# Turning the last three pairs' inputs by DMA, whole-run loads for a range test, and a new instruction order

## The chip, the core and the metric

The kernel runs on one core of one Trainium2 chip. A core has engines with a queue each, which run side by side and wait for one another through semaphores: TensorE (PE: matrix products, with its weight loads shown as PEld), VectorE (DVE), ScalarE (ACT) and GpSimd (POOL); SyncE (SP) issues DMAs here. Each queue is worked off in order: an instruction that waits holds up all that stand behind it on its engine. The metric is the device time of the program in microseconds (us), as the median of the runs.

## The reference

Two blocks follow one another. The first is a gated linear attention with complex gates, for 4 batches, 8 heads, 768 tokens and head width 48:

```python
mag = np.sqrt(a_re * a_re + a_im * a_im)
scale = np.minimum(mag, 0.999) / (mag + 1e-06)
a_re_n, a_im_n = (a_re * scale, a_im * scale)
for t in range(S):
    new_re = ar * S_re - ai * S_im
    new_im = ar * S_im + ai * S_re
    S_re, S_im = (new_re + kv, new_im)        # kv = outer product of k[t] and v[t]
    y[:, :, t] = np.einsum('bhd,bhde->bhe', q[:, :, t], S_re)
```

Its output, with the heads side by side (384 columns), is x of a mixer: `h = x^T U V` mixes along the tokens through rank 32, `u = x + h^T`, and the result is `u + relu(u w1) w2` with 1536 hidden columns. The weights come in as float64, the rest as float32.

## The kernel before

**Work and stages.** The recurrence is done in 24 chunks of 128 tokens, 6 for each batch, and two neighbouring chunks are a group (12 groups). For a group, `gates` (L690) computes from a_re and a_im the logarithms of the magnitudes and the angles, sums them along the tokens with TensorE (`within`, L777; `angles`, L842), and makes scale factors (es) and cosines and sines (cs). The phase at the end of a chunk is carried into the next one of its batch: in batch 0 by TensorE, later (from chunk 7 on) by a small adding DMA on POOL's queue (L828, "gate<-F" in the profile), behind which VectorE's cast of L836 waits. `prep` (L880) multiplies q and k by these. From chunk 6 on (`ACROSS`) `cross` (L919) turns the products by DMA: ScalarE splits each 32-bit word into two 16-bit planes (L932), SP writes them to DRAM (L933), and a transposing DMA reads them back (L934). `chain` (L938) does the chunk's attention: inner products (L956), key-value states (L976), outputs (L1005, L1013), into the tile xo of the chunk.

When the six chunks of a batch are through, `mixer` (L1029) runs for its three pairs of chunks (12 pairs in all, m = 0 to 11). The rank products (L1048) of the batch are kept by ScalarE as r (L1054). For a pair, `spread` (L1063) multiplies r by V into two banks of PSUM (L1071, one TensorE operation for both chunks), `mixed` (L1076) adds them to xo on VectorE, and `turned` (L1080) turns xo for the up-projection: three transposes on TensorE for each chunk (L1087), and one copy out of PSUM into the tile uT (L1091). uT has two buffers. Pair 0 is turned and up-projected ahead of its batch's end, and a correction by the rank (`ranked`, L1116 and L1124, with ScalarE's copy at L1128, and `corrected`, L1142) brings in the mixing later. Its weights and those of the other pairs come in as 64-bit words, which ScalarE and VectorE make into 32-bit ones in passes (`single`, L589) in the first 110 us or so. From pair 2 on the up-projection is `up_fewer` (L1163): sums of blocks of uT on VectorE (L1186), then 15 groups of 8 TensorE instructions ("few" and "bank", L1214), with copies and additions of the parts on ScalarE and VectorE. `down_two` (L1311) does the down-projection in 14 halves of 6 instructions (L1346), adds to xo (L472) and sends the result out (L1290).

**The range test.** The fast path holds for a range of the gates alone. `again` (L665) reads a_re and a_im a second time for every group, into the places that the gates have left: four loads by SP (two arrays, two chunks, 128 tokens x 8 heads x 48 values in runs of 192 bytes; L671), a square on ScalarE (L674), and two VectorE operations (`ranged`, L658: L660 and L661) that leave a count in `bad`; `low` is a place to write for the second. `judge` (L1480) looks at the counts at the end. The test needs every value once, in any arrangement.

**What sets the order.** The program is planned before it is emitted. Each call of `PE`, `ACT`, `DVE`, `POOL` or `SP` enters an operation with what it reads and writes; the buffers are taken and given back by the plan (`takes`, rings). The tuple `ORDER` then lists all 2276 operations by their number in the order in which they are emitted, and so fixes the order in each engine's queue. `SPARE` and `WARM` add matmuls without a use ahead of the operations they name (L1506, L1513). The costs, `late`, `way` and `steps` in these calls are notes for whoever makes ORDER; they do not reach the program.

Of the kernel before, what the change touches and what calls it, by code (L numbers as in the profile page):

```python
# [10 lines left out]
FP = mybir.dt.float32  # L11
# [8 lines left out]
CH = 128  # L20
# [98 lines left out]
)  # L119

SPARE = {
    410: 3, 447: 1,
}

WARM = {
# [201 lines left out]
def kernel(  # L327
# [125 lines left out]
    def SP(cost, *a, **kw):  # L453
        plan.add("SP", 0.63, *a, late=cost, **kw)
# [1128 lines left out]
```

## Time and profile before

| | |
|---|---|
| median of 3 runs | 530.15 us (529.94 to 530.81) |
| the profiled execution | 529.77 us |
| its span, first to last instruction | 528.0 us |
| mean granted TensorE clock | 0.997 |
| busy: PE, DVE, ACT, POOL | 509.3, 414.5, 346.0, 31.6 us |
| HBM read and written | 43.03 and 23.63 MB |

The page of the profile gives busy times, groups of instructions by line with their mean duration in ns, the idle time ahead of them and what ended it, and the chain of waits: from the last instruction back, at each step to what released it. Matmuls are pipelined: the mean duration of one is longer than the time by which it moves the chain on, so for TensorE the pieces of the chain (start, length, what) are read, not the means. Times in rows are us from the start of the span unless ns stands beside them. A busy TensorE need not be at its peak.

### The profile page before, as it was taken

The numbers are of one execution on the slowest core, as the hardware profiler recorded it, in microseconds if no ns is written. First come the engines' busy times: TensorE is split into PE (matmuls) and PEld (weight loads), VectorE is DVE, ScalarE is ACT, GpSimd is POOL, SyncE is SP. The second block draws the span as 40 slices with busy tenths as digits, with TensorE's granted clock in tenths as the row PEclk, the third lists the DMA queues.
The fourth block names the chain that finished last, engine by engine and source line by source line (L and its number), as shares of the span: only waits on it lengthen the run. The fifth ranks groups of instructions, "written<-read, shape, count | busy, mean of one in ns | idle before, by whom it ended". The sixth has DMA issues, their size and how long they took to land.

```text
span 528.0 us, 15692 instructions
## 1 busy us (share of the span) xinstructions
PE 509.3 (96%) x6670; PEld 460.3 (87%) x6670; DVE 414.5 (79%) x787; ACT 346.0 (66%) x555; POOL 31.6 (6%) x61
## 2 busy tenths in 40 slices
PE   4999999899999999999999999999999999999996
PEld 2777887666998997999999989999999989999996
DVE  4779897799989987898798797878796575958452
ACT  8899998998869978978896768843543313131100
POOL 1000000001010000101011000110000000000110
PEclk9999999999999999999999999999999999999998
DMA  9959958479999998999899958999897543333101
GB/s 226 173 115 270 209 115 191 140 138 217 197 215 244 216 215 145 204 217 202 205 198 227 210 144 175 170 242 229 192 217 178 108 90 61 76 60 61 39 32 35
DMA packets 280670, 87.06 MB, mean 165 GB/s; under 512 B 271288, under 2 KB 272784, under 8 KB 280592
## 3 DMA queue, kind: packets, MB, share of 16 engines
q1 hardware_dynamic: 278384, 81.63, 76.0%
q0 software_dynamic: 2208, 4.35, 2.4%
q8 instruction: 54, 0.88, 0.7%
q14 instruction: 24, 0.20, 0.1%
HBM read 43.03 MB, written 23.63 MB: 126 GB/s over the span
## 4 chain that ended last, share of the span: by engine, by line
PE 88%; ACT 5%; DMA 3%; DVE 2%; issue 1%; SPq 0%; ACTq 0%
PE down L1346 25%; PE few L1214 14%; PE bank L1214 11%; PE up L1102 6%; PE inner L956 4%; PE bank L1013 4%; PE bank L976 4%; PE down L1303 3%; PE bank L1005 2%; DMA gate<-F 2%; PE bank L1071 2%; PE bank L1087 2%; ACT gate L466 1%; PE bank L777 1%; PE bank L782 1%; PE bank L842 1%
## 5 line engine op out<-in xcount | busy, mean ns | idle before, releaser
L466 ACT ACTIVATE gate<-gate 128x768 f32<-128x768 f32 (+2 forms) x85 | 86.1, 1018 | 25.8 <-DMA gate<-in_a_im_dram 14.7
L1346 PE MATMUL down<-w,h 128*128 128x192 f32 x396 | 70.4, 328 | 0.0
L466 ACT ACTIVATE QK<-QKC 128x768 uint16<-128x768 uint16 (+1 forms) x72 | 58.5, 848 | 13.1 <-DVE QKC L469 7.9
L1346 PEld LDWEIGHTS down<-w,h 128*128 128x128 f32 x396 | 64.6, 190 | 1.2 <-issue 0.8
L469 DVE TENSOR_TENSOR QKC<-qk,cs 128x768 f32<-128x768 f32 x48 | 44.9, 952 | 1.0 <-ACT cs L466 0.6
L472 DVE TENSOR_TENSOR xo<-down,xo 128x192 f32<-128x192 f32 (+1 forms) x79 | 29.9, 385 | 14.3 <-PE down L1346 14.1
L1222 ACT COPY h<-few 128x512 f32<-128x512 f32 x35 | 20.2, 583 | 27.8 <-PE few L1214 27.6
L1222 ACT COPY h<-bank 128x512 f32<-128x512 f32 x25 | 14.3, 588 | 36.0 <-PE bank L1214 31.0
L1346 PE MATMUL down<-stage 128*128 128x192 f32 x198 | 37.2, 328 | 0.0
L1102 PE MATMUL up<-uT,w 128*128 128x256 f32 x144 | 33.8, 383 | 0.0
L1346 PEld LDWEIGHTS down<-stage 128*128 128x128 f32 x198 | 32.5, 190 | 0.3 <-issue 0.2
L1102 PEld LDWEIGHTS up<-uT,w 128*128 128x128 f32 x144 | 26.7, 190 | 4.9 <-issue 0.6
L1290 POOL DMA_DIRECT2D out_dram<-xo x32 | 18.5, 590 | 202.9 <-DVE xo L472 164.5
L463 ACT ACT_TABLE_LOAD x22 | 28.2, 1283 | 1.1 <-PEq L1567 0.7
L828 POOL DMA_DIRECT2D gate<-F x15 | 12.0, 797 | 274.7 <-DVE stage L616 86.3
L1226 DVE CUSTOM_DVE_ANT_1 h<-few,h 128x512 f32<-128x512 f32 x31 | 21.0, 686 | 8.8 <-PE few L1214 8.1
L1214 PE MATMUL few<-extra,w 128*128 128x128 f32 x216 | 27.8, 275 | 0.0
L956 PE MATMUL inner<-QK 112*64 112x64 f32 x768 | 27.5, 224 | 0.2 <-DVE AT L959 0.2
L466 ACT ACTIVATE cs<-F 128x384 f32<-128x384 f32 x48 | 24.4, 518 | 3.9 <-DVE F L851 3.7
L956 PEld LDWEIGHTS inner<-QK 112*64 112x64 f32 x768 | 24.5, 138 | 2.4 <-issue 0.8
L1214 PEld LDWEIGHTS few<-extra,w 128*128 128x128 f32 x216 | 26.3, 192 | 0.1
L466 ACT ACTIVATE es<-bank 128x384 f32<-128x384 f32 x44 | 18.4, 502 | 9.2 <-PE bank L777 8.2
(185 smaller groups left out, 1166.8 us busy)
## 6 DMA issues: line engine op xcount, KB each, us to landing
xd<-QK SPq DMA_DIRECT2D x36, 512.0 KB
gate<-in_a_re_dram SPq DMA_DIRECT2D x48, 192.0 KB
gate<-in_a_im_dram SPq DMA_DIRECT2D x48, 192.0 KB
stage<-in_moe_w_ch_dram SPq DMA_DIRECT2D x12, 768.0 KB
qk<-in_q_dram SPq DMA_DIRECT2D x24, 192.0 KB
qk<-in_k_dram SPq DMA_DIRECT2D x24, 192.0 KB
VP<-in_v_dram SPq DMA_DIRECT2D x24, 192.0 KB
out_dram<-xo POOLq DMA_DIRECT2D x12, 192.0 KB, 4.2
```

Source lines behind the costliest of these rows:

```text
L463: ACT(1.37, rank, lambda: nc.scalar.preload_act_table_set(name), writes=[TABLE])
L466: return nc.scalar.activation(out=o, in_=i, func=f, **kw)
L469: nc.vector.tensor_tensor(out=o, in0=a, in1=b, op=OP.mult)
L472: nc.vector.tensor_tensor(out=o, in0=a, in1=b, op=OP.add)
L956: nc.tensor.matmul(out=get(*ps0)[r:r + HC, h], lhsT=k_of(h, r, HC), rhs=q_of(h, r, HC), start=True, stop=True, tile_position=(0, r))
L976: nc.tensor.matmul(out=get(*dk[r])[x:x + D, h], lhsT=get(*ks)[at, h, x // DP, 0:D], rhs=get(*VPi)[at, h], start=True, stop=True, tile_posi ...
L1013: nc.tensor.matmul(out=get(*y[u])[side(r, u), p], lhsT=q_of(h, r * HC, HC), rhs=get(*(mid_G if r else ("G", i - 1)))[:, h], start=False, s ...
L1102: nc.tensor.matmul(out=get(*ps)[:, e], lhsT=w1[:, f, (ff + e) * 128:(ff + e + 1) * 128], rhs=get(*uT)[:, f], start=(f == 0), stop=(f == KD ...
L1214: nc.tensor.matmul(out=get(*ps)[:, q], lhsT=w()[:, q * 128:(q + 1) * 128], rhs=v[0](), start=(n == 0 and q == 0), stop=True, skip_group_ch ...
L1222: ACT(c_act(n3 * CH) - 0.045, RU, lambda i=i, k=k: nc.scalar.copy(out=at(i, k), in_=get(*ps)), [ps], [o])
L1226: DVE(c_dve(n3 * CH), RU, lambda i=i, k=k: nc.vector._custom_dve(dve_ops.TENSOR_ADD_SAT, out=at(i, k), in0=get(*ps), in1=at(i, k), s0=math ...
L1346: nc.tensor.matmul(out=get(*to)[:, part], lhsT=x(j), rhs=y[:, j], start=(first and j == 0), stop=(j == KH - 1), skip_group_check=not first)
```

## The change

Four things change. For the pairs m = 9, 10 and 11 (chunks 18 to 23) `turned` calls the new `across`: two ScalarE operations split xo into 16-bit planes in XU (one tile, a ring of one buffer), SP writes the planes to DRAM (six places) and issues a transposing DMA that writes the chunk's part of uT. Their three transposes and the copy go. `again` loads a group's a_re and a_im with one DMA each, in runs of 3072 bytes, and `low` holds 16-bit numbers. The operation of `spread` no longer takes a buffer of uT; the turn does. ORDER is a new list of 2264 operations, with other SPARE and WARM.

```diff
 ORDER = (
...
 SPARE = {
-    410: 3, 447: 1,
+    403: 1, 410: 1, 416: 1, 422: 1, 447: 1,
 }
 WARM = {
-    112: (2, 1), 126: (1,), 136: (2, 2, 2, 2, 2, 2, 1), 141: (2,), 162: (2, 2, 2), 235: (2, 2, 2, 2, 1), 242: (2,), 245: (2,), 259: (2, 2, 1), 266: (1, 1, 1, 1, 1, 1, 1, 1, 1),
+    125: (2, 2, 1), 126: (1,), 136: (2, 2, 2, 2, 2, 2, 1), 140: (2, 2), 163: (2, 1), 187: (2,), 201: (1,), 235: (2, 2, 1), 239: (2,), 242: (2,), 245: (2, 1), 259: (2, 2, 2, 1, 1, 1, 1, 1), 263: (1,),
 }
...
-    low = singles.tile([128, GC * DM], FP, name="low")
+    low = singles.tile([128, GC * DM], U16, name="low")
+    XU = singles.tile([128, 2, DM], U16, name="XU")
...
+    TURNED = (9, 10, 11)
...
-        for (nm, src), i in ((a, i) for a in ((ar, a_re), (ai, a_im)) for i in range(lo, hi)):
-            SP(c_dma(DM), ("load", 30 + n), lambda nm=nm, src=src, i=i: nc.sync.dma_start(out=get(*nm)[:, i - lo], in_=rows(src, i)),
-               writes=[nm + (i,)])
         flat4 = lambda a: get(*a).rearrange("p c h d -> p (c h d)")
+        b, c = where(lo)
+        for nm, src in ((ar, a_re), (ai, a_im)):
+            SP(c_dma(W), ("load", 30 + n), lambda nm=nm, src=src: nc.sync.dma_start(
+                out=flat4(nm), in_=src[b, :, c * CH:(c + hi - lo) * CH].rearrange("h t d -> h (t d)").rearrange("h (p m) -> h p m", m=W)), writes=[nm])
...
-            PE(0.76, R0, products, [r, ("V", 0)] + [uT + ("kept",)] * (m >= AHEAD), ps, way=5, steps=8)
+            PE(0.76, R0, products, [r, ("V", 0)], ps, way=5, steps=8)
...
+            if m in TURNED:
+                across(cc, i, u)
+                return
...
-            PE(0.33, R0, turn, [u], [tr], steps=KD)
+            PE(0.33, R0, turn, [u], [tr], takes=[uT], steps=KD)
...
+        def across(cc, i, u):
+            xu, xv = ("xu", i), ("xv", i)
+            ring(xu, "xu", [XU])
+            buffer(xv, "XV", 6, [CH, DM], bass.MemoryType.DRAM)
+            for n in range(2):
+                ACT(c_act(DM), R0, lambda n=n: act(get(*xu)[:, n], get(*u).bitcast(U16).rearrange("p (m n) -> p m n", n=2)[:, :, n], AF.Copy),
+                    [u], [xu + (n,)])
+            SP(0.6, R0, lambda: nc.sync.dma_start(out=get(*xv).bitcast(U16), in_=get(*xu).rearrange("p n m -> p (n m)")), [xu], [xv])
+            SP(0.8, R0, lambda: nc.sync.dma_start_transpose(
+                out=get(*uT).rearrange("p f (c t) -> p f c t", c=MC)[:, :, cc].bitcast(U16),
+                in_=get(*xv).bitcast(U16).rearrange("t (n m) -> (t n) m", n=2)), [xv], [uT + (cc,)])
```

Where the new order puts things that matter here: behind the rank products of batch 3 come one group of pair 8's up-projection, pair 9's mixing products, three more such groups, the mixing products of pairs 10 and 11, and twelve halves of pair 8's down products, and then pair 9's first up-projection group. Pair 9's transposing DMAs, the write of chunk 20 and the transposing DMA of chunk 20 stand on SP in that order with two range loads among them. Behind the rank products of batch 1 come two state products (L976) ahead of the mixing products. In batch 0 an up product (L1102) that stood between the rank products and L1116 is now earlier.

174 rows, old and new, of the table ORDER are left out of this document.

## The prediction

> **What bounds the kernel now.** I read the page first, then the waits of TensorE, then the stages, then the chain of waits.
>
> ```profile
> PE 509.3 (96%) x6670; PEld 460.3 (87%) x6670; DVE 414.5 (79%) x787; ACT 346.0 (66%) x555; POOL 31.6 (6%) x61
> ```
>
> TensorE (PE) is busy for 96% of the 528.0 us. A busy PE can still stand and wait behind a pipelined matmul, so the waits come next (total, times, longest, in us).
>
> ```profile
> PE bank L782 <- DVE GL L742: 7.7, 1, 7.7
> PE up L1142 <- ACT more L1128: 2.1, 1, 2.1
> PE down L1346 <- DVE xo L472: 1.1, 1, 1.1
> PE down L1346 <- DVE stage L1338: 0.7, 1, 0.7
> PE bank L1071 <- ACT r L1054: 0.6, 1, 0.6
> ```
>
> The 7.7 us are the start, before there is anything to multiply. After that four waits are worth naming, 4.5 us in all. That is all that a better order can win back from idle PE; more has to come from less PE work.
>
> ```profile
> 0.00:40.00 40.00, 31.14 (x287) 22.33 (x288) 26.28 (x51) 35.02 (x57) 1.94 (x14) 1.00 0.87 172
> 40.00:80.00 40.00, 39.96 (x815) 32.19 (x813) 35.70 (x56) 38.73 (x71) 0.00 (x0) 1.00 0.85 200
> ...
> 440.00:480.00 40.00, 40.00 (x319) 39.55 (x318) 27.50 (x61) 9.57 (x17) 0.54 (x1) 1.00 0.42 77
> ```
>
> The columns are the stage and its length, then PE, PEld, DVE, ACT and POOL busy, the granted clock (1.00: nothing more to be had there), the DMA share, GB/s. There are three regimes: up to 40 us ScalarE (35.02 of 40) sets the pace; from 40 us PE does, with ScalarE almost as full (38.73); late, PE alone is full, and ScalarE (9.57) and the DMA engines (0.42) have room.
>
> The chain of waits agrees: from 284 us to the last down products it is PE, piece upon piece; the rows of (1) are some of them (start, us, what). A PE instruction removed late shortens the span by its own length, as long as nothing new makes PE wait.
>
> **The change part by part.** (1) **Six turns leave PE.** Chunks 18 to 23 lose their three transposes each. These are the six in the chain, between pieces of other work that I need below:
>
> ```profile
> 431.79 0.33 PE bank L1087 x3
> 432.12 0.98 PE down L1346 x6
> 433.10 0.33 PE bank L1087 x3
> ...
> 445.43 0.33 PE bank L1087 x3
> 445.76 0.89 PE few L1214 x8
> ...
> 453.07 0.85 PE bank L1071 x8
> 453.92 0.48 PE bank L1087 x3
> ...
> 465.94 0.66 PE bank L1087 x6
> ```
>
> 0.33 + 0.33 + 0.33 + 0.48 + 0.66 = 2.13 us, all on the chain: **-2.1 us**. [...]
>
> What comes instead: two ScalarE splits for each chunk, and two DMAs on SP's queue. The nearest rows are a ScalarE pass over 384 columns, the mixing addition, the stores of tokens (96 and 192 KB; one chunk's write to DRAM is 192 KB too), and the transposing DMAs that the kernel has already (8 blocks each, the new ones have 3):
>
> ```profile
> L466 ACT ACTIVATE cs<-F 128x384 f32<-128x384 f32 x48 | 24.4, 518 | 3.9 <-DVE F L851 3.7
> ```
> ```profile
> L472 DVE TENSOR_TENSOR xo<-bank,xo 128x384 f32<-128x384 f32 x24 | 12.8, 551 | 4.0 <-issue 2.3 <-PE bank L1071 1.7
> ```
> ```profile
> L1290 POOL DMA_DIRECT2D out_dram<-xo x32: 539/539/859, 127.7 to 509.7; - x32
> ...
> DMA to landing us min/median/max: 1.9/3.5/6.1
> ```
> ```profile
> L934 SPq DMA_TRANSPOSE QK<-xd x36: 1732/2794/4559, 119.3 to 407.5; - x36
> ```
>
> ScalarE gains 12 x 0.52 us and loses six copies of about 0.48: +3.4 us, in a stage where it has 30 of 40 us free: nothing. The latency matters. XU is one buffer, so the second chunk's splits wait until the first chunk's write has landed. For pair 9, from the end of its mixing products: addition 0.55, splits 1.04, write 3.5, splits 1.04, write 3.5, transposing DMA about 1.0 (3/8 of 2.79) to issue and 3.5 to land, two small additions at most 0.6: 14.7 us. The transposing DMA's landing does not show in the trace; I give it the stores' median, and bound it by 1.9 and 6.1. The cover is counted in the new order: between these products and pair 9's first up-projection PE has three "few" groups (0.89), two more mixing products (0.85) and twelve halves of pair 8's down products (0.98): 2.7 + 1.7 + 11.8 = 16.2 us. So it is hidden with 1.5 us to spare; each us beyond that is a us of PE. Queued behind on SP are range loads, which nobody on the path waits for; behind the blocked splits on ScalarE stand range squares, and pair 9's own copies. Pairs 10 and 11 have over 25 us of PE between their mixing and their first use. Their transposes stand behind range loads on SP, which wait for the test before (DVE), but 15 us or more of PE lies there too. Cost: 0, from both sides -0 and +7 (all three landings at 6.1 give 22.5).
>
> (2) **Range tests.** 48 loads become 24 of the same bytes in long runs.
>
> ```profile
> L671 SPq DMA_DIRECT2D gate<-in_a_re_dram x24: 367/582/1881, 319.6 to 477.7; - x24
> ```
>
> The first is issued at 319.6 us, where PE has no wait left, so the saved DMA time is worth 0; it only keeps SP freer for (1). The test's output in 16 bits changes a DVE instruction off the path: 0, bounds 0.
>
> (3) **The mixing products no longer take the uT buffer.** They may run earlier, and do: pairs 10 and 11 are mixed right after pair 9. It adds no work; two PSUM banks are held longer, at a time when the chains of the last pairs use others. 0.
>
> (4) **The new order.** Two waits above come from one mechanism:
>
> ```profile
> 151.00 6.34 DMA gate<-F
> ...
> 157.37 0.37 DVE GS L836
> ```
> ```profile
> 275.81 6.09 DMA gate<-F
> ```
> ```profile
> DMA to landing us min/median/max: 1.9/3.9/6.3
> ```
>
> The phase carried from chunk to chunk is added by a DMA (L828; last fence: its landings). VectorE stands at the cast behind it, and what PE needs is queued there. In the old order PE has only 2.9 us of its own work between chunk 10's phase and chunk 11's cast, 2.8 before chunk 17's. The new order puts 4.9 and 7.3 us there. But chunks 7, 19 and 21 come down to 3.7 to 3.9, less than the landing's median of 3.9 alone. Of 1.1 + 0.7 = 1.8 us I count **-1.2**; bounds -1.8 and +1.0.
>
> ```profile
> 86.53 1.78 PE rank L1048 x16
> 88.31 1.49 PE up L1102 x6
> ```
> ```profile
> 208.43 0.49 ACT r L1054
> ...
> 208.96 1.57 PE bank L1071 x16
> ```
> ```profile
> L466 ACT ACTIVATE stage<-stage 128x768 uint16<-128x768 uint32 x7 | 7.7, 1099 | 2.0 <-DVE w L472 2.0
> ```
>
> After a batch's rank products PE needs ScalarE's copy r. In batch 1 nothing lies between (0.55 us lost); the new order puts two state products there: **-0.55**. In batch 0 an up product covers the copy today (second row); the new order moves it away and leaves one filler matmul, and on ScalarE a 1.1 us weight pass stands ahead of the copy. Rank's last round (half of the first row, 0.9) covers part: 1.1 + 0.5 - 0.9 = **+0.7**; bounds 0 (the pass is early) and +1.6 (nothing covers). The 2.1 us before L1142 stay: ScalarE still has four operations between r and that copy. Start, tail and the other stages: 0, with bounds of 1.5 us either way, since ScalarE and VectorE are nearly full up to 300 us and their queues are all reshuffled.
>
> Sum: 528.0 - 2.13 - 1.2 - 0.55 + 0.7 = 524.8 us of span. The profiled execution took 529.77, 1.77 outside its span, and lies 0.38 under the median of the three runs: 524.8 + 1.77 + 0.38 = **527.0 us**.
>
> **Rivals.** (A) *The gains are eaten again.* At 93 us the new order puts four ScalarE operations (a table load, a copy, two weight passes) ahead of the copy that L1142 needs, the last behind a 768 KB load issued only just before. If that load lands 3 us late, PE waits 3 us longer, and the result is about 530.0: no difference. For it: the 2.1 us there now. Against it: in the old order five operations stand there.
>
> (B) *Pair 9 comes too late: slower.* If the three landings take 6.1 us each, the way is 22.5 us against 16.2 of cover: PE waits 6.3 us and the time is 533.3. It turns slower from the point where the wait exceeds the 3.2 us won and 1.1 more, that is at landings of 5.4 us on average instead of 3.5. For it: the maximum was measured, and there is one XU buffer. Against it: the DMA share is only 0.42 there. [...]
>
> (C) *The reshuffled first 300 us lose: slower.* ScalarE is 38.73 of 40 us full from 40 to 80; an operation queued wrongly shows at once on PE. Were the 4.5 us of waits to double, the sum would be -2.1 + 4.5 = +2.4: 532.5. For it: two places already change sign by 0.7 us. Against it: the new order leaves most inputs about as far ahead of their PE work as before, counted in PE work.
>
> (D) *A transpose is worth what it takes by itself.*
>
> ```profile
> L1087 PE MATMUL bank<-ident,xo x72: 271/273/329, 45.9 to 466.3; 128*128 128x128 f32 x72
> ```
>
> Then 18 of them give 18 x 0.273 = 4.9 us instead of 2.1, and the time is 524.2. Against it: the pieces of the chain above. [...]
>
> **How the numbers follow.** About 0.2% (1.1 us) is what a measurement of this kernel can tell from no change. Forecast 527.0: 0.53, itself between 525.3 and 529.0. A: 0.17. B: 0.11. C: 0.14. D: 0.05. Faster: forecast and D and a little of A, 0.60. The same: the rest of A and the near end of C, 0.16. Slower: B and most of C, 0.24. The range runs from close to D, which is also where the good ends of (4) lead (-2.1 - 1.8 - 0.55 and 1 us of the start: 524.7), 524.5, to the middle of C and the near part of B, 532.0.
>
> **What would show it.** Right: no L1087 after 430 us and a span of about 525; PE full from 430 us to the end, no wait of DVE's L1186 or of "few" for a DMA; a smaller idle time of L836 behind gate<-F; L1071 without a wait for r in batch 1, and a new wait of L1116 for r in batch 0. Wrong: a gap of PE ahead of pair 9's first "few" (B); a longer wait of L1142 (A); PE less than 39 of 40 us busy between 40 and 300 us (C). The end of the last down products would move with the span in each case.

## The result, and the profile after

The changed kernel takes **543.18 us** (median of 6 runs, 542.12 to 547.83) beside 530.13 us for the kernel before (6 runs on the same chip): ratio **1.0265** with a 95% interval of 1.0223 to 1.0307. It is 13 us slower; 527.0 us was forecast, and the range ended at 532.0. The profiled execution took 542.12 us, 2.2 of them outside its span of 539.9. In what follows, medians are over all runs of a kernel, but ratios leave out runs more than 1.5% above its fastest, so the two do not match for e2, e5 and e6, and e2's ratio rests on two runs (555.20 and 562.77 us) while its trace is of a run of 564.05 us.

In the changed kernel the lines have moved by 2 to 18: L671 of before is L675, L836 is L839, L1071 is L1074, L1087 is L1093, L1116 is L1134, L1142 is L1160, L1346 is L1364; the new DMAs of the turned inputs are L1108 (write to DRAM) and L1109 (transposing). The waits of TensorE, as shown of before (total, times, longest, in us):

```profile
PE bank L785 <- DVE GL L745: 7.9, 1, 7.9
PE down L1364 <- DVE xo L472: 3.9, 3, 1.6
PE bank L845 <- DVE stage L618: 1.5, 1, 1.5
PE inner L959 <- issue: 1.4, 1, 1.4
PE bank L1232 <- ACT h L1240: 1.3, 1, 1.3
PE bank L979 <- issue: 0.9, 1, 0.9
```

The start is as it was. ("issue" means that the trace names nothing that ended the wait.) The waits that the prediction wanted to win are gone: those of 1.1 and 0.7 us behind the carried phase and that of L1071 for r. The 2.1 us before L1142 (now L1160), which it had left standing, are gone from the list too, but that product starts at 99.77 us where it started at 95.97 before, so this is no gain. And there are new waits. Most of them lie after 340 us, where before there were none: 1.34 and 1.57 us of L1364 for xo (its third, 1.0 us, lies at 197 us), and those of L959, L1232 and L979. The table by stage, first one row of the kernel before, then three of the changed kernel (stage and its length, then PE, PEld, DVE, ACT and POOL busy, granted clock, DMA share, GB/s):

```profile
360.00:380.00 20.00, 20.00 (x215) 19.95 (x206) 17.03 (x37) 9.33 (x17) 1.07 (x2) 1.00 1.00 202
```
```profile
360.00:380.00 20.00, 18.40 (x261) 17.29 (x260) 15.88 (x36) 8.23 (x15) 2.49 (x4) 1.00 0.82 202
...
420.00:440.00 20.00, 18.59 (x297) 15.93 (x296) 13.18 (x23) 6.05 (x14) 0.00 (x0) 1.00 0.42 105
...
480.00:500.00 20.00, 18.68 (x141) 18.49 (x141) 12.99 (x29) 3.23 (x5) 0.54 (x1) 1.00 0.50 89
```

TensorE was busy for 20.00 of 20 us in each of the three before. What ended the waits stands in the chain of waits. The first and the second load here are two of the whole-run range loads, the third is the one behind a transposing DMA (start, us, what):

```profile
348.45 8.10 DMA gate<-in_a_re_dram
...
356.58 0.06 DVE gate L662
...
364.26 7.90 DMA gate<-in_a_re_dram
...
372.18 0.96 DVE gate L662
```
```profile
477.48 1.24 SPq L1109
...
478.81 7.17 DMA gate<-in_a_im_dram
...
486.00 0.03 ACT gate L466
...
486.75 1.06 ACT h L1240 x2
...
487.86 3.84 PE bank L1232 x32
```

In the first fence a test on VectorE (gate, L662) stands until its load has landed, 8.10 and 7.90 us after the issue, and TensorE's waits of 1.34 us at 358 us and 1.57 us at 372 us for xo come behind it. Read the second fence from the bottom: TensorE waits for a ScalarE copy h (L1240); the copy stands in ScalarE's queue behind the square of a range test (gate, L466); the square waits for its load, which takes 7.17 us from its issue; and the load itself was issued only when SyncE (SP) had got rid of a transposing DMA (L1109). Nobody needs the range test before the end of the kernel. But an engine takes its instructions in order, so what stands behind the test waits as if it needed it.

Another place lies early. These are two stages of the same table behind the wait of L845, which lies at 87 us; the granted clock is the last column but two:

```profile
88.00:92.00 4.00, 3.43 (x70) 2.99 (x73) 2.10 (x4) 1.21 (x3) 0.96 (x1) 0.62 0.61 200
92.00:96.00 4.00, 4.00 (x24) 1.83 (x24) 0.00 (x0) 3.23 (x6) 0.00 (x0) 0.53 0.94 179
```

TensorE stands for 1.49 us, and then works at half its clock until about 96 us. A count of the work done (every matmul of both traces at the median step to its successor in the trace of before) puts the changed kernel some 3.5 us behind at 100 us and 11 to 13.5 us at 480 us. Between these it moves by up to 5 us with the way in which the work is priced, so it says only that most is lost late. Of the first 3.5 us, about 1.7 are owed to the execution that is compared with: the kernel before has its wait of 2.1 us at 93 us, and in its profiled execution no half clock followed, while 3.4 us or more at half the clock followed the same wait in all nine other traces with the old order at the start (mean granted clock 0.981 to 0.996 over their spans, 0.997 in before).

### The profile page after: what moved, and what is told of

It reads as the page before. It is cut to its first block, busy times and chain, and to the rows that moved or that the text cites. A ratio compares the mean times of both kernels' runs of the same rounds, so it can differ in the third digit from the quotient of the medians.

```text
span 539.9 us, 15623 instructions
## 1 busy us (share of the span) xinstructions
PE 515.0 (95%) x6654; PEld 461.5 (85%) x6654; DVE 415.5 (77%) x787; ACT 349.8 (65%) x561; POOL 32.0 (6%) x61
## 4 chain that ended last, share of the span: by engine, by line
PE 71%; DVE 9%; DMA 8%; ACT 7%; issue 2%; SPq 2%; DVEq 0%; ACTq 0%
PE down L1364 22%; PE few L1232 12%; PE bank L1232 9%; PE up L1120 4%; PE inner L959 3%; PE bank L1016 3%; DMA gate<-in_a_re_dram 3%; PE bank L979 3%; ACT gate L466 2%; DMA gate<-in_a_im_dram 2%; PE bank L1008 2%; PE bank L785 2%; PE bank L1074 2%; DMA QK<-xd 1%; SPq L937 1%
## 5 line engine op out<-in xcount | busy, mean ns | idle before, releaser
L466 ACT ACTIVATE gate<-gate 128x768 f32<-128x768 f32 (+2 forms) x85 | 85.9, 1015 | 20.6 <-DMA gate<-in_a_im_dram 13.6
L466 ACT ACTIVATE QK<-QKC 128x768 uint16<-128x768 uint16 (+1 forms) x72 | 59.0, 850 | 20.4 <-DVE QKC L469 19.8
L1364 PE MATMUL down<-w,h 128*128 128x192 f32 x396 | 70.3, 328 | 0.0
L1364 PEld LDWEIGHTS down<-w,h 128*128 128x128 f32 x396 | 64.7, 190 | 1.2 <-DVE h L1244 0.5
L1364 PE MATMUL down<-stage 128*128 128x192 f32 x198 | 36.8, 329 | 2.4 <-DVE xo L472 2.4
L1364 PEld LDWEIGHTS down<-stage 128*128 128x128 f32 x198 | 32.3, 190 | 3.3 <-DVE xo L472 2.9
L1240 ACT COPY h<-bank 128x512 f32<-128x512 f32 x25 | 14.3, 587 | 29.6 <-PE bank L1232 29.5
L1240 ACT COPY h<-few 128x512 f32<-128x512 f32 x35 | 20.1, 585 | 18.3 <-PE few L1232 18.0
L959 PE MATMUL inner<-QK 112*64 112x64 f32 x768 | 27.6, 224 | 2.1 <-issue 1.4
L959 PEld LDWEIGHTS inner<-QK 112*64 112x64 f32 x768 | 24.5, 138 | 5.1 <-issue 3.2
L1232 PE MATMUL few<-extra,w 128*128 128x128 f32 x216 | 28.4, 278 | 0.0
L1232 PEld LDWEIGHTS few<-extra,w 128*128 128x128 f32 x216 | 26.1, 192 | 1.3 <-issue 0.6
L466 ACT ACTIVATE cs<-F 128x384 f32<-128x384 f32 x48 | 23.8, 519 | 3.0 <-DVE F L854 3.0
L466 ACT ACTIVATE es<-bank 128x384 f32<-128x384 f32 x44 | 18.5, 496 | 11.1 <-PE bank L780 8.9
```

The source lines that it names most:

```text
L466: return nc.scalar.activation(out=o, in_=i, func=f, **kw)
L959: nc.tensor.matmul(out=get(*ps0)[r:r + HC, h], lhsT=k_of(h, r, HC), rhs=q_of(h, r, HC), start=True, stop=True, tile_position=(0, r))
L1232: nc.tensor.matmul(out=get(*ps)[:, q], lhsT=w()[:, q * 128:(q + 1) * 128], rhs=v[0](), start=(n == 0 and q == 0), stop=True, skip_group_ch ...
L1240: ACT(c_act(n3 * CH) - 0.045, RU, lambda i=i, k=k: nc.scalar.copy(out=at(i, k), in_=get(*ps)), [ps], [o])
L1364: nc.tensor.matmul(out=get(*to)[:, part], lhsT=x(j), rhs=y[:, j], start=(first and j == 0), stop=(j == KH - 1), skip_group_check=not first)
```

## The experiments

Theories: **(1)** the whole-run loads land late and hold up the engines in order (with a form 1a: it is the queue behind them; 1b: they take other transfers' time; 1c, added after e4: they run on half of the DMA engines); **(2)** the order costs, whatever the loads; **(3)** the wait at 87 us and the clock behind it. Two came later: **(4)** what e4 loses is queues behind an instruction that waits; **(5)** TensorE's instructions come too late in a dense block. Ratios are to the kernel before, run beside it on the same chip.

| | kernel | median us | ratio, 95% interval |
|---|---|---|---|
| e1 | changed, short range loads | 534.84 | 1.0039 (1.0006 to 1.0073) |
| e2 | changed, tests later | 563.41 | 1.0509 (1.0433 to 1.0585) |
| e3 | changed, product of angles later | 546.60 | 1.0285 (1.0232 to 1.0339) |
| e4 | before, two pairs by DMA, close | 549.05 | 1.0328 (1.0292 to 1.0363) |
| e5 | changed, loads in 16 pieces | 534.89 | 1.0064 (1.0038 to 1.0091) |
| e6 | e1 with turns on TensorE | 540.30 | 1.0147 (1.0094 to 1.0200) |
| e7 | before, two pairs by DMA, spaced | 529.96 | 0.9975 (0.9952 to 0.9998) |
| e8 | before, whole-run loads | 533.18 | 1.0041 (1.0014 to 1.0068) |
| e9 | e5, old order to 320 us | 532.59 | 1.0009 (0.9979 to 1.0040) |
| e10 | e5, old order to 125 us | 533.30 | 1.0026 (1.0000 to 1.0052) |
| e11 | e7, loads in 16 pieces | 529.47 | **0.9962 (0.9941 to 0.9983)** |
| e12 | e9 with the change's own loads | 540.95 | 1.0165 (1.0119 to 1.0211) |
| e13 | e9, dense blocks spread | 532.28 | 1.0015 (0.9992 to 1.0037) |
| e14 | e9 with turns on TensorE | 536.81 | 1.0108 (1.0072 to 1.0143) |

**e1, the loads put back.** In the place of each whole load:

```diff
-            SP(..., lambda: nc.sync.dma_start(out=flat4(nm), in_=src[b, :, c * CH:(c + hi - lo) * CH]...), writes=[nm])
+            SP(..., lambda: [nc.sync.dma_start(out=get(*nm)[:, i - lo], in_=rows(src, i)) for i in range(lo, hi)], writes=[nm])
```

> The changed kernel (median 543.18) with one thing put back: each whole range load is again two loads of one chunk each, in the same place of the order. Theory 1, the long loads are late: in the changed kernel's trace two range loads issued together land 7 to 8 us after their issue (348.45 to 356.58, 364.26 to 372.18, 478.81 to 485.98), VectorE or ScalarE stand behind them, and TensorE has gaps of 1.34, 1.57 and 1.32 us there; without them 4.2 us or more come back: 536 to 539, and the three gaps are gone. Theory 2, the new order costs whatever the loads are, the loads nothing, as the prediction's step (2) had it: 542.5 to 544, and the gaps stay.

The time falls by 2.3% (1.0265 to 1.0039), some 12 us: theory 1, and more than expected. In its trace the waits of 1.34 us at 358 and 1.32 us at 486 are gone and the 1.57 us at 372 are 0.30. The turns and the order stayed as they were, so neither of them makes the 13 us by itself.

**e2, the tests later.** Only the order changes: square, square-sum and test of a group up to 45 places behind its second load.

```diff
 ORDER: for each group of range loads
-    load, load, square, square-sum, test (0 to 56 places behind the second load)
+    load, load, ... square, square-sum, test (up to 45 places behind, or just ahead of the next load)
```

> The changed kernel with its whole loads, but each group's three range operations (square, square-sum, test) stand later in the order, up to 45 places behind the second load, where the next load leaves room. Theory 1a, it is the in-order queues behind a late load that cost: about what the small loads give, 537 to 540. Theory 1b, the long transfers hold up other transfers and that costs: no more than 1 us comes back, 542 to 544. Theory 2 (order alone, not the loads): 542.5 to 544.

A miss for all theories: 1.0509, slower by another 2.4%. The chain of waits in its trace shows one reason (the wait of TensorE that it ends with is 5.6 us long):

```profile
506.92 0.98 DVE low L666 x2
...
507.91 0.60 SPq L678
...
508.56 5.47 DMA uT<-xv
```

The next range load may not start before the test has read its buffer, so SyncE stands at that load (L678, for 13.4 us) until the moved test is done, and pair 11's transposing DMA stands behind it on SyncE. Moving the test freed VectorE and blocked SyncE. Theory 1a is not refuted by this, since the move has a cost of its own, but it isn't shown by it either.

**e3, the product of angles later.**

```diff
 ORDER, TensorE around 87 us
-    chain (y, 4), angles (ph, 6), chain inside 5, chain (y, 5), chain (y, 5), rank k 1
+    chain (y, 4), chain inside 5, chain (y, 5), chain (y, 5), angles (ph, 6), rank k 1
```

> The changed kernel with one TensorE operation moved: the product of angles of chunk 6 stands again behind the last product of chunk 5's chain, three TensorE operations later, as in the kernel before. Theory 3, a wait and the clock: in the changed kernel's trace TensorE stands 1.49 us before this product at 87 us, and the granted clock is 0.50 from about 89 to 95 us; with neither, 1.5 us and about 3 us (half of 6 us) come back in part: 538.5 to 541, granted clock above 0.99. Rival: the wait only moves to the next operation that needs the angles, and the clock drops anyway: 542.5 to 544.

The rival was right: no gain (1.0285, inside the interval of the changed kernel). The wait has only moved, and the clock falls as before:

```profile
PE bank L1011 <- ACT xo L1030: 1.6, 1, 1.6
```
```profile
92.00:96.00 4.00, 4.00 (x18) 0.91 (x18) 1.94 (x3) 3.18 (x8) 0.96 (x1) 0.58 0.89 165
```

The trace puts the wait down to a PSUM bank that ScalarE had still to empty (xo), but that copy ended at 87.52 us, 0.8 us before the product started. The changed kernel, e1, e2, e3, e5 and e6 share this start of the order, and in all six traces TensorE stands here for 1.5 to 1.9 us, whichever operation comes next. Each of these waits ended 1.3 to 1.5 us after a 16 KB packet of the instruction queue had. So it is not shown that ScalarE is what is late; e13 and the last section come back to waits of this kind.

**e4, two pairs in the old order.** The kernel before, with the transposes of pairs 10 and 11 done as in the change (`TURNED = (10, 11)`), each write and transposing DMA right behind its splits; the 16-bit `low` comes with it. 

> The kernel before with one part of the change: the inputs of pairs 10 and 11 (four chunks, twelve transposes) are turned by DMA, in the old order, with the old range loads. By step (1) of the prediction each transpose is worth what it moves the chain: 0.33 + 0.48 + 0.66 = 1.47 us: 528.7, ratio 0.9972. Rival, the single price of 0.273 us each: 3.3 us, 526.9. Rival, the new ScalarE and DMA work holds something else up: 530.1 or more.

It is 3.3% slower, with two waits of TensorE of 6.0 and 8.6 us. The way to the first of them:

```profile
440.11 0.95 ACT XU L470 x2
...
441.07 1.88 DMA xv<-XU
...
442.98 1.21 SPq L1112
...
444.23 3.65 DMA gate<-in_a_re_dram
...
447.90 0.97 DVE gate L666
```

SyncE holds the transposing DMA (L1112) until the write has landed; the range load stands behind it, the test behind the load, and behind the test on VectorE stand the sums that TensorE needs. This is the same way as at 477 us in the changed kernel.

**e5, the loads in 16 pieces.** A long load alone keeps the DMA engines busy for about half of their time (share 0.53, first two rows below). One word of its source was changed:

```diff
-... .rearrange("h t d -> h (t d)").rearrange("h (p m) -> h p m", m=W)
+... .rearrange("h t d -> h (t d)").rearrange("h (p m) -> p h m", m=W)
```

> The changed kernel with its whole range loads, the same bytes in the same 3072-byte runs, but the source written with its 16 pieces per head outermost and the 8 heads inside, instead of 8 heads outermost (which row lands on which partition changes, and the tests do not care). In the changed kernel's trace a long load alone keeps the DMA engines busy for 0.40 to 0.56 of their time, the share of 8 of 16. Theory 1c, a transfer is dealt to the engines by its outermost dimension, so the long loads run on half of them: now on 16, share near 1, the landing of a pair falls from 7 to 8 us to 4 to 5, and the time to about that of the short loads, 533 to 537. Rival, the long runs themselves are slow, however dealt: 542 to 546.

Theory 1c: 1.0064, so 2.0% (1.5 to 2.5) come back from the order of two dimensions. Stages in which hardly anything but such a load runs, of the changed kernel and then of e5 (the last two columns are the DMA share and GB/s):

```profile
425.00:429.00 4.00, 4.00 (x123) 3.84 (x118) 1.32 (x2) 1.73 (x6) 0.00 (x0) 1.00 0.53 154
482.20:484.70 2.50, 2.50 (x24) 2.50 (x24) 1.74 (x3) 0.59 (x1) 0.00 (x0) 1.00 0.53 118
```
```profile
419.30:421.80 2.50, 2.50 (x72) 2.39 (x72) 0.25 (x1) 1.73 (x6) 0.00 (x0) 1.00 0.98 272
484.70:486.00 1.30, 1.30 (x10) 1.30 (x9) 0.83 (x2) 0.65 (x1) 0.00 (x0) 1.00 1.01 260
```

From 118 to 260 GB/s. In the packets of the traces 8 of a load's 3072-byte packets are under way at any time in the changed kernel and 16 in e5, and a pair of loads issued together has its last packet done 6.3 to 8.2 us after the first issue in the one (groups from 410 us on) and 4.8 to 5.4 us in the other. So about half of the 16 DMA engines work on such a load in the changed kernel (share 0.53), and all of them in e5 (0.98 to 1.01). The one difference in the code is that the source has its 8 heads outermost in the one and the 16 pieces of a head in the other; how other shapes are dealt is not shown.

**e6, turns on TensorE again.** e1 with `TURNED = ()`, transposes and copies at the places of the transposing DMAs, pair 11 mixed later. 

> The changed kernel with the short range loads (as in the first experiment, 534.84) and also with the last three pairs turned on TensorE again, each transpose and its copy at the place of the transposing DMA, pair 11 mixed later as the PSUM banks need. By the prediction's step (1) this costs 2.1 us: 536.5 to 537.5. If the turned inputs, with their waits on SyncE and ScalarE, give back what they win: 533 to 535.

1.0147 against 1.0039: the turns by DMA are worth 1.1% in the new order (0.5 to 1.7 by the two intervals), 2 to 9 us, together with the later mixing of pair 11. They win, by the medians more than either forecast had it; the size stays wide.

**e7, two pairs, spaced.** e4 with twelve operations at other places: each write and each transposing DMA on SyncE where what it waits for has had time, the splits on ScalarE likewise. 

> The kernel before with pairs 10 and 11 turned by DMA in the old order, as in the fourth experiment, but each write and each transposing DMA placed on SyncE's queue where what it waits for has had time, so that the range loads behind it and ScalarE's copies behind the splits are not held up. Theory 4, that experiment lost its 17 us to queues behind a waiting instruction (6.0 and 8.6 us of TensorE's waits, and the half clock after each): the waits go and the 1.47 us of the transposes remain as a gain: 528.5 to 529.5. Rival, the turned inputs cost that wherever they stand: above 535.

0.9975 (0.9952 to 0.9998): 1.3 us faster, where 1.47 were forecast for these twelve transposes, and the two waits of e4 are gone. The same instructions in other places of the queues make 19 us (1.0328 against 0.9975).

**e8, whole-run loads in the old order.** 

> The kernel before, old order, turns on TensorE, but each pair of range loads of one chunk each replaced by one whole load as in the change, issued at the place of the first of the two. If the long loads cost by themselves, landing late wherever they are: 533 to 540. If they only cost with the new order, where the tests stand too close behind them: 529.5 to 531.

1.0041: they cost 2.2 us there (0.7 to 3.6), by the ratio between the two answers. Its engines wait even longer for these loads than those of the changed kernel; the first two rows are of e8, the next two of the changed kernel:

```profile
ACT gate L466 <- DMA gate<-in_a_im_dram: 17.8, 7, 5.7
DVE gate L660 <- DMA gate<-in_a_re_dram: 5.7, 3, 3.0
```
```profile
ACT gate L466 <- DMA gate<-in_a_im_dram: 13.6, 5, 7.1
DVE gate L662 <- DMA gate<-in_a_re_dram: 8.0, 3, 3.3
```

In the kernel before, with short loads, the same two rows are 14.7 and 4.7 us. So it isn't the waiting that counts. In e8's trace TensorE waits only once after 320 us (0.6 us, and not for a load); in the changed kernel it waits for 6.5 us. That the difference is what stands behind the waiting instruction is read from the chains above.

**e9, e10, e12: which part of the order.** The old order for everything that the new one has ahead of its first range load (320 us) or ahead of the product of angles of chunk 8 (125 us), the new order after it.

> The changed kernel with the long loads dealt over 16 pieces (as in the fifth experiment, ratio 1.0064) and the old order for everything that the new order has before its first range load at about 320 us, the old fillers too; the new order after that, with all three pairs turned by DMA. If the first 320 us of the new order are what is left of the loss (1.9 to 5.7 us behind the kernel before at 320 us in the traces of the four kernels that share them): 527 to 530, ratio 0.993 to 0.999. If the loss that is left is in the last 200 us: 533 to 536.

> As the ninth, but the old order only up to the product of angles of chunk 8 (about 125 us), the new order after that. If the wait of 1.5 to 1.7 us at 87 us and the half clock behind it are the loss of the first 320 us: as the ninth, within 1 us. If the new order loses between 130 and 320 us instead (waits of 0.5 at 166 and 1.0 us at 197 us): 3 us more than the ninth, as much as the fifth (ratio 1.006).

> As the ninth, but with the change's own loads (8 heads outermost, 8 engines). If what the long loads cost (2.0% in the new order, 0.4% in the old one) is made in the new order's last 200 us, where the tests stand closer behind them: 10 us more than the ninth, 537 to 541. If it takes the disturbed first 320 us as well: 2 to 4 us more than the ninth.

e9 is 0.55% below e5 (0.1 to 1.0): the first 320 us of the new order cost about 3 us. e10 lies between, and isn't told apart from either. e9 came out near 532.6, between its two forecasts; the last 200 us of the new order eat what the turns win. e12 against e9: 1.6% (1.0 to 2.1), 8 us, for the change's own loads in place of those in 16 pieces, with the first 320 us in the old order. So most of what the long loads cost comes without the disturbed start.

**e11, the best of it.** Old order, two pairs by DMA, loads in 16 pieces. 

> The kernel of the seventh experiment (old order, pairs 10 and 11 turned by DMA, ratio 0.9975) with the range loads whole and dealt over 16 pieces. The loads' DMA time was never on TensorE's path in the old order: 0 to -1 us against the seventh, ratio 0.9955 to 0.9980. If a load of long runs is late even on 16 engines: 1.000 or more.

0.9962 (0.9941 to 0.9983): 2.0 us faster than the kernel before, and 16 us faster than the changed one. It is not told apart from e7 (0.9975), so what the 16-piece loads add there is not shown.

**e13, e14: what is lost after 340 us, and what a transpose is worth.** In e9 two waits are left there, and nothing that the trace names ends them; the first is shown with what surrounds it:

```profile
PE bank L978 <- issue: 2.4, 2, 1.6
```
```profile
386.40 0.57 PE bank L978 x34
386.98 1.64 issue
...
389.26 2.22 PE down L1363 x6
```

The six down matmuls behind the wait take 2.22 us in place of 0.98: the half clock again (granted 0.52 from 389 to 392.5 us). A 16 KB packet of the instruction queue ended at 387.1 us. The blocks ahead of such waits are 266 to 284 short matmuls and weight loads in 4 us.

> The ninth experiment's kernel (ratio 1.0009) with four TensorE operations moved: three products of chunk 20's chain go between the last few-products of pair 7, and one few-product of pair 8 goes into chunk 21's chain, so that fewer short matmuls follow each other. Theory 5, instructions come too late for a dense block: the waits of 1.64 us at 387 and 0.74 us at 408 us shrink or go, 1 to 3 us come back: ratio 0.995 to 0.999. Rival, the waits have another cause, or move with the instructions: 1.000 to 1.002.

The rival: 1.0015 (0.9992 to 1.0037), no gain. Both waits are gone, and one of 1.9 us stands in their place at 414 us, with the half clock behind it (mean granted clock 0.992, as in e9's trace):

```profile
PE inner L958 <- issue: 1.9, 1, 1.9
```

> The ninth experiment's kernel (ratio 1.0009) with the last three pairs turned on TensorE again, in the places of the transposing DMAs. By step (1), 2.1 us of TensorE come back: 1.0045 to 1.006. If the turned inputs cost as much as they win (waits on SyncE and ScalarE): 1.000 to 1.002. If each transpose were worth its own 0.273 us: 1.010.

1.0108 against 1.0009: the 18 transposes and the later mixing of pair 11 that goes with them here are worth 1.0% (0.5 to 1.5), 2.8 to 7.7 us.

## Why the prediction was wrong, step by step

**Step (2) failed**, with the sentence of step (1) that leans on it. Step (2) said that the first long load "is issued at 319.6 us, where PE has no wait left, so the saved DMA time is worth 0", with bounds of 0 on both sides; step (1) said of SyncE's queue: "Queued behind on SP are range loads, which nobody on the path waits for". Both looked at who needs the data. The cost came from who stands behind the instruction that waits. Bounds of 0 were the mistake that made the range too narrow: the changed transfer, 384 KB in 3072-byte runs with 8 heads outermost, shows nowhere in the trace of before, so its landing should have been bounded from the nearest rows and carried to the queues behind it. e5 and e1 take 2.0 and 2.3% off by the loads alone, 11 and 12 us. That nothing urgent depends on the tests was true, and no help.

**Step (1), the turns**, was right in its kind. The transposes are gone late (last start 383.3 us, 54 in place of 72):

```profile
L1093 PE MATMUL bank<-ident,xo x54: 270/273/329, 46.4 to 383.3; 128*128 128x128 f32 x54
L1109 SPq DMA_TRANSPOSE uT<-xv x6: 1207/1221/1235, 439.8 to 489.9; - x6
```

No wait of TensorE for pair 9's input appears, so the cover was enough and rival B did not come true. (The second row is the time that SyncE spends on each transposing DMA.) The way was shorter than forecast: in e4's chain the write of a chunk landed 1.88 us after its splits, both times, where 3.5 were taken. The 3.5 us are the median landing of stores that GpSimd issues (L1290 of before); these writes are issued by SyncE. For twelve transposes in the old order the price by the chain, 1.47 us, agrees with e7 (1.3, interval 0.1 to 2.5); the 3.3 us of rival D lie outside it. For eighteen in the new order e14 gives 2.8 to 7.7 us, above the 2.1 and around D's 4.9. In e14's chain a turn again takes 0.33 us (three of the four pieces between 430 and 495 us; the fourth takes 0.55), which speaks for the price of step (1) and for the move of pair 11's mixing. It isn't settled which of the two makes the difference.

**Step (3)** was not tried alone.

**Step (4), the order**: the two waits behind the carried phase and the wait of batch 1 went as forecast; VectorE's cast, which waited 4.3 us for gate<-F before, does not wait for it in the changed kernel. The forecast wait of batch 0 is not in its list. But the step also put the rest of the first 300 us at 0, with 1.5 us either way, and **this zero was too low as well**: about 3 us are measured (e5 to e9, 0.5 to 5.3). What was not foreseen is the wait at 87 us, just ahead of the place that was worked out. The chain leads over ScalarE (L463 is the table load) and VectorE:

```profile
82.72 1.28 ACT L463
...
84.02 0.85 ACT gate L466
...
84.89 0.85 ACT gate L466
...
85.77 0.37 DVE GS L839
...
86.16 0.56 DVE GS L840
...
87.65 0.52 DVE stage L618
88.17 0.39 issue
88.57 0.52 PE bank L845 x2
```

But the product L845 does not read `stage`, a pass over weights. It reads the two halves of GS (L839, L840), which were there at 86.72 us; its first weight load ran at 87.01 us, and then nothing until 88.57. In e1 the trace names nothing for the same wait (1.7 us, "issue"). So this wait is of the kind that e13 moved, and its cause is as open. **Rival C** had the place (the first 300 us) and 4.5 us for it. One of its signs is there, TensorE being 38.32 of 40 us busy from 160 to 200 us (39.98 before), with a wait of 1.0 us at 197 us behind a load of q that SyncE issued only after 4.08 us at a transposing DMA. For the wait at 87 us its mechanism (ScalarE full, an operation queued wrongly) is not shown. With 11 us for (2) and 3 us here the forecast would have been 541. **Rival A** did not happen: the wait of L1142 is gone. But the order did not win it, for the product starts 3.8 us later than before, behind the wait at 87 us.

Put together by the ratios: long loads on half of the DMA engines 2.0% (changed to e5), first 320 us of the new order 0.55% (e5 to e9), and 0.1% left (e9), in which the gain of the turns and a loss of the new order's last 200 us cancel. That loss shows in the traces of e9 and e13 as waits for no named cause and the half clock behind them; e13 moved it and did not remove it, so its cause is open. Part of the 2.0% is the clock. An estimate from the granted clock and the span of each run (the share not granted, taken off the span) leaves the changed kernel 6.0 us above e5, and e12 6.9 us above e9; 3.5 and 1.3 us more are half clock. The record does not show how much of that follows waits for loads and how much the early wait, which lies before any range load: after it the clock was halved for 6.8 us in the changed kernel's trace and not at all in e5's.

## What to carry to other kernels

Before pricing a transfer at nothing because its result isn't urgent, list what stands behind its consumer on each in-order engine, and behind its issuer, and look whether that work is urgent: e4 and e7 differ by 19 us in nothing but such places. When a transfer is reshaped, look at the order of its dimensions and at the DMA share in the trace: here longer runs on half of the DMA engines (share 0.53) cost 2.3% more than short runs (e1), and dealt over all of them (0.98 to 1.01) 2.0% less than on half (e5). A change that carries a new order is best tried part by part, old order first; here two pairs by DMA with loads in 16 pieces win 0.4% in the old order, and the change as it came loses 2.65%.

## What the runs showed of the hardware that was not expected

- Runs of 3072 bytes dealt over 8 heads moved 118 GB/s in a stretch with hardly anything else (DMA share 0.53), the same runs with 16 pieces outermost 260 GB/s (1.01).
- Waits of TensorE of 1.5 to 2.1 us were followed by half its clock for 3.4 us or twice that: at 87 us in the changed kernel (6.8 us), at 387 us in e9 (3.4 us). It doesn't always come. The wait at 87 us was followed by 6.8 us at half the clock in three of six traces, by 3.4 in two, and by none in e5's, where it lasted 1.7 us. The same code and a wait of 2.1 us at 93 us were followed by 1.00 in the profiled run of before and by 0.60 in e11's:

```profile
92.00:96.00 4.00, 1.89 (x19) 0.99 (x11) 1.63 (x4) 3.98 (x6) 0.00 (x0) 1.00 0.79 225
96.00:100.00 4.00, 4.00 (x19) 2.92 (x16) 3.25 (x6) 3.02 (x4) 0.00 (x0) 0.60 0.47 180
```

  Each 3.4 us at half the clock are 1.7 us of work.
- Inside blocks of 266 to 284 short matmuls and weight loads within 4 us (L976 of before, L979 of the changed kernel) TensorE stood for 0.4 to 1.6 us with nothing to wait for, in fifteen of the sixteen traces, and each of these waits ended 1.2 to 1.6 us after a 16 KB packet of the instruction queue had. The six waits at 87 us, with 238 to 240 in the 4 us ahead of them, ended 1.3 to 1.5 us after one. That instructions came too late is argued from this, not shown: the waits of 2.1 us at 93 us ended 1.3 to 1.8 us after such a packet too, and there the copy that TensorE needed ended just then (95.92 us in before, the product started at 95.97). Of the waits of the same kind between two groups, three (the 1.9 us at 414 us in e13 is one) ended 1.1 us after such a packet, and the 1.4 us at 423 us in the changed kernel ended before one had: that one has no explanation here.
